# One core, five engine queues in another order: a gated recurrence with a gated convolution layer

## The chip, the cores and the metric

The kernel runs on one core of a Trainium2 chip. Its engines each work through a queue of their own in order: TensorE (PE; its weight loads are listed apart as PEld), VectorE (DVE), ScalarE (ACT), GpSimd (POOL) and SyncE (SP), which here only issues DMAs. An instruction waits at the head of its queue until the instructions that it depends on, on other engines, have signalled. The metric is the device time in microseconds (us) of one launch, as the median of several runs.

## The reference

The inputs are `x`, `r_gate` and `i_gate`, each 4 x 6336 x 256 in float32, and small weights. For every channel, with `k = 8 log(clip(sigmoid(a_param)))`:

```python
a_t = exp(k * sigmoid(r_gate))
u_t = sqrt(max(1 - a_t * a_t, 1e-6)) * sigmoid(i_gate) * x
h_t = a_t * h_(t-1) + u_t                 # along the 6336 steps of each batch
gate = sigmoid(sum_k conv_w[k] * h_(t-4+k))   # 5 taps, causal, per channel
out = (gate * (h @ w_val)) @ w_out        # both weights 256 x 256
```

The output is again 4 x 6336 x 256 in float32.

## The kernel before

The four batches are one row of 25344 steps. It is cut into 51 windows (`w`, 256 or 512 steps) and 28 chunks (`c`): chunks 0, 1, 2, 26 and 27 are one window each (0, 1, 2, 49 and 50), and every other chunk is two windows of 512 (chunk 3 is windows 3 and 4, chunk 25 is windows 47 and 48). Loads bring steps to partitions; PE transposes bring channels to partitions, in two halves (`h` 0 and 1), for the recurrence. All sigmoids are made from Tanh, so that Tanh and Exp use one activation table; Sqrt needs another, and each change between them is a table load (L501).

No scheduler decides the order. One long string, `ORDER`, names every piece of work as a word, and the loop at L496 emits the words in turn (`@` gives the PSUM banks). An engine's queue is therefore the words of that engine in the order of the string. The words, by engine:

- SP: `lr.w`, `li.w`, `lx.w` load a window of `r_gate`, `i_gate` and `x` (0.5 MB each for 512 steps); `st.w` stores a window of the output; `s_wl` loads weights.
- ACT: `th.w` Tanh of both gates of a window (L290); `ex.c.h` Exp that gives `a` for a group of one or two chunks (L342); `rt.b` Sqrt for a batch of one to three chunks (L369; batch 3 is chunks 3 and 4, batch 4 is chunks 5 to 7, batch 11 the last two); `tg.w` Tanh of the convolution (L441); `sa.c.h` a square of `a` (L358); `ca.w.0` copy of a result from PSUM (L474).
- POOL: `pp.w` adds 1 to the Tanh of the input gate, in place (L298); `up.w` multiplies that by `x` (L310); `sq.c.h` a square of `a` (L350).
- DVE: `uv.w` does both steps of `pp` and `up` at once, as two instructions of half a window each (one for 256 steps; L315); `sv.c.h` a square of `a` (L354); `xg.w` multiplies by the root (L389); `sc.c.h` the recurrence as a scan, one per half (L422); `gv.w` gate times value (L454); `cd.w.0` copy of a result from PSUM (L472).
- PE: `tr`, `nt`, `xt` transposes (L326, L382, L400); `cv.w` convolution by diagonal matrices (L434); `vl.w` and `ou.w` the two products (L449, L464).

So the gated input of a window comes from `pp` and `up` on POOL or from `uv` on DVE, and a square from `sq` on POOL, `sv` on DVE or `sa` on ACT, as `ORDER` has it.

What one window needs, in turn: `lr`, `li` -> `th` -> `tr` -> `ex` -> `sq`/`sv`/`sa` -> `rt` -> `nt`; `th` and `lx` -> `pp`, `up` or `uv`; both -> `xg` -> `xt` -> `sc` -> `cv` -> `tg` and `vl` -> `gv` -> `ou` -> `cd`/`ca` -> `st`. Buffers are rings, and a word also waits until its slot is free. The rings that matter here: `riring`, four windows (`lr.w` and `li.w` wait for `th.(w-4)`); `xring`, four windows (`lx.w` waits for the `up` or `uv` of w-4); `tring`, three windows, whose part for the input gate is single (`th.w` waits for the `up` or `uv` of w-3); `tgring`, three windows; `oring`, four windows.

The two ways to the gated input:

```python
def op_up(w):                                   # POOL, after op_pp(w)
    u, t1, xt = u_args(w)
    nc.gpsimd.tensor_tensor(out=u, in0=t1, in1=xt, op=ALU.mult)

def op_uv(w):                                   # DVE
    u, t, xt = u_args(w)
    for q in range(wins[w] // (2 * P)):
        nc.vector.scalar_tensor_tensor(out=u[:, q], in0=t[:, q], scalar=1.0, in1=xt[:, q],
                                       op0=ALU.add, op1=ALU.mult)
```

Of the kernel before, what the change touches and what calls it, by code (L numbers as in the profile page):

```python
# [532 lines left out]
```

## Time and profile before

| what | value |
|---|---|
| median of 3 runs | 303.58 us (302.06, 303.58, 303.75) |
| the profiled execution's own time | 301.82 us |
| its span (first to last instruction) | 300.0 us |
| busy: ACT, DVE, PE, POOL | 281.7, 260.6, 238.4, 209.6 us |
| moved by DMA | 104.75 MB, 349 GB/s over the span |
| ACT words: th, ex, rt, tg, sa, ca | 51, 38, 12, 51, 6, 18 |

The difference between the profiled execution's time and its span lies outside the traced instructions. "Busy" is the time in which an engine had an instruction of its own in work; starts of neighbours on one engine lie a little closer than the durations, so sums of durations come out slightly above the time that they take. A group's mean duration, the idle time before it, and what ended that idle time are what the rows of the profile give.

### The profile page before, as it was taken

To read this page: it belongs to the slowest core of one execution; us is meant where nothing else is said; L and a number is where in the kernel's file an instruction comes from. 1 tells how busy PE (TensorE), PEld (TensorE's weight loads), DVE (VectorE), ACT (ScalarE), POOL (GpSimd) and SP (SyncE) were. 2 spreads that over 40 slices of the span, in tenths; PEclk is the share of its full clock that TensorE was granted. 3 is DMA by queue.
4 is the path that set the end of the run, shared out by engine and by line. 5 is a ranking of instruction groups with operands and counts; after the bars stand their busy time and mean duration, and the time that the engine had idled before them with its cause. 6 is when DMAs were issued, how large, how long until landed. Compare 5 with 4: busy or idle time off the path is not lost.

```text
span 300.0 us, 6281 instructions
## 1 busy us (share of the span) xinstructions
PE 238.4 (79%) x2487; PEld 165.2 (55%) x2487; DVE 260.6 (87%) x241; ACT 281.7 (94%) x203; POOL 209.6 (70%) x137
## 2 busy tenths in 40 slices
...
GB/s 258 408 410 398 397 390 409 386 378 375 392 391 381 385 378 415 415 376 374 410 416 409 415 416 413 305 357 405 303 418 407 318 315 316 263 42 137 214 125 246
DMA packets 29996, 104.75 MB, mean 349 GB/s; under 512 B 3335, under 2 KB 3854, under 8 KB 29966
## 3 DMA queue, kind: packets, MB, share of 16 engines
...
q14 instruction: 11, 0.09, 0.1%
...
## 4 chain that ended last, share of the span: by engine, by line
ACT 29%; PE 24%; DVE 20%; DMA 16%; issue 9%; SPq 1%; ACTq 0%; DVEq 0%
DMA riring<-in_i_gate_dram 14%; ACT tring L290 9%; DVE yring L422 9%; PE banks L464 7%; ACT ering L369 6%; PE banks L434 6%; ACT tgring L441 6%; PE banks L449 5%; ACT aring L342 5%; DVE tgring L454 4%; PE banks L382 3%; DVE uring L389 3%; DVE oring L472 3%; PE banks L400 2%; ACT L501 2%
## 5 line engine op out<-in xcount | busy, mean ns | idle before, releaser
L350 POOL TENSOR_TENSOR ering<-aring 128x1024 f32<-128x1024 f32 (+2 forms) x48 | 85.7, 1803 | 38.9 <-ACT aring L342 38.6
L422 DVE TENSOR_TENSOR_SCAN yring<-aring,yring,banks 128x1024 bf16<-128x1024 f32 (+5 forms) x54 | 106.4, 1990 | 1.0 <-ACT aring L342 0.5
L290 ACT ACTIVATE tring<-riring 128x2048 bf16<-128x2048 f32 (+1 forms) x51 | 93.5, 1865 | 3.5 <-DMA riring<-in_i_gate_dram 2.6
L310 POOL TENSOR_TENSOR uring<-tring,xring 128x1024 bf16<-128x1024 bf16 (+1 forms) x39 | 81.7, 2110 | 3.9 <-PE banks L434 1.7
L434 PE MATMUL banks<-yring,diag 64*64 64x512 bf16 (+7 forms) x1080 | 65.5, 371 | 5.1 <-DVE oring L472 3.5
L454 DVE SCALAR_TENSOR_TENSOR tgring<-tgring,banks 128x1024 bf16<-128x1024 bf16 (+1 forms) x51 | 59.7, 1181 | 4.3 <-ACT tgring L441 2.1
L464 PE MATMUL banks<-wo,tgring 128*128 128x256 bf16 x396 | 52.1, 277 | 8.1 <-DVE tgring L454 6.2
L342 ACT ACTIVATE aring<-banks,khf 128x2048 f32<-128x2048 bf16 (+3 forms) x38 | 54.4, 1473 | 0.7 <-PE banks L326 0.6
L441 ACT ACTIVATE tgring<-banks 128x1024 bf16<-128x1024 f32 (+1 forms) x51 | 49.6, 1005 | 4.6 <-PE banks L434 3.4
L449 PE MATMUL banks<-yring,wv 128*128 128x512 bf16 (+4 forms) x216 | 51.6, 367 | 2.7 <-ACT tgring L441 0.9
L464 PEld LDWEIGHTS <-tgring 128*128 128x128 bf16 x396 | 42.0, 115 | 18.5 <-DVE tgring L454 11.1
L382 PE MATMUL banks<-ident,ering 128*128 128x128 f32 x198 | 31.7, 306 | 23.0 <-ACT ering L369 22.3
L298 POOL TENSOR_SCALAR tring<-tring 128x1024 bf16<-128x1024 bf16 (+1 forms) x39 | 39.6, 1028 | 14.2 <-ACT tring L290 14.0
L434 PEld LDWEIGHTS <-diag 64*64 64x64 bf16 x1080 | 30.0, 108 | 32.2 <-issue 17.5
L369 ACT ACTIVATE ering<-ering 128x4096 bf16<-128x4096 f32 (+5 forms) x15 | 45.0, 3019 | 0.1
L382 PEld LDWEIGHTS banks<-ident,ering 128*128 128x128 f32 x198 | 28.0, 209 | 27.5 <-ACT ering L369 23.0
L389 DVE TENSOR_TENSOR uring<-banks,uring 128x1024 bf16<-128x1024 bf16 (+1 forms) x51 | 31.8, 666 | 10.0 <-PE banks L382 9.4
L472 DVE COPY oring<-banks 128x1024 f32<-128x1024 f32 (+1 forms) x33 | 38.6, 1178 | 2.0 <-PE banks L464 1.9
L326 PE MATMUL banks<-ident_b,tring 128*128 128x128 bf16 x396 | 29.2, 229 | 13.0 <-ACT tgring L441 6.0
L326 PEld LDWEIGHTS <-tring 128*128 128x128 bf16 x396 | 25.3, 103 | 19.1 <-issue 11.8
L449 PEld LDWEIGHTS <-wv 128*128 128x128 bf16 x216 | 19.8, 99 | 23.0 <-issue 10.3
L315 DVE SCALAR_TENSOR_TENSOR uring<-tring,xring 128x512 bf16<-128x512 bf16 x23 | 17.4, 823 | 13.1 <-DMA xring<-in_x_dram 10.7
...
## 6 DMA issues: line engine op xcount, KB each, us to landing
...
```

The costliest lines, as they stand in the source:

```text
L290: nc.scalar.activation(out=tring[:, w % NTRI, a:a + 2, 0:J, :], in_=riring[:, w % NRI, :, 0:J, :], func=ACT.Tanh, scale=0.5)
L310: nc.gpsimd.tensor_tensor(out=u, in0=t1, in1=xt, op=ALU.mult)
L342: nc.scalar.activation(out=dst, in_=src, func=ACT.Exp, scale=khf[:, h:h + 1], bias=khf[:, h:h + 1])
L350: nc.gpsimd.tensor_tensor(out=e, in0=a, in1=a, op=ALU.mult)
L369: nc.scalar.activation(out=ering[:].bitcast(BF16)[:, 4 * o:4 * o + 2 * n], in_=ering[:, 2 * o:2 * o + 2 * n], func=ACT.Sqrt, scale=-0.25, ...
L382: nc.tensor.transpose(out=bank[:, (q * H + h) * P:(q * H + h + 1) * P], in_=ering[:, o + h * clen[c] // 2 + q:o + h * clen[c] // 2 + wins[ ...
L422: nc.vector.tensor_tensor_scan(out=yring[:, h, col:col + o1 - o0], data0=aring[:, h, a_at[c] + o0:a_at[c] + o1], data1=xT[:, o0:o1], initi ...
L434: nc.tensor.matmul(out=gp[oh * 64:oh * 64 + 64, h, a:b], lhsT=diag[half * 64:half * 64 + 64, h, k, :], rhs=yring[half * 64:half * 64 + 64, ...
L441: nc.scalar.activation(out=tgring[:, w % NTG, :, 0:wins[w]], in_=live.pop(("gp", w))[:, :, 0:wins[w]], func=ACT.Tanh, scale=0.5)
L449: nc.tensor.matmul(out=val[:, m, a:b], lhsT=wv[:, hk, m * P:(m + 1) * P], rhs=yring[:, hk, col:col + b - a], start=(hk == 0), stop=(hk == ...
L454: nc.vector.scalar_tensor_tensor(out=tgring[:, w % NTG, :, 0:wins[w]], in0=tgring[:, w % NTG, :, 0:wins[w]], scalar=1.0, in1=live.pop(("va ...
L464: nc.tensor.matmul(out=ops[:, j * D:(j + 1) * D], lhsT=gv[:, hk, j:wins[w]:J], rhs=wo[:, hk, :], start=(hk == 0), stop=(hk == H - 1))
```

## The change

Only the string `ORDER` changes; all functions stay as they are, `uv` and its two instructions included. The new string is a new search's result, in which the two halves of `uv` are counted as separate steps between which POOL may take its turn. It has 993 words instead of 990:

- `pp` and `up` on POOL now make the gated input of windows 3, 5, 6, 8 and 11, which `uv` on DVE made before; `uv` makes that of windows 14 and 36, which were POOL's. DVE has 9 `uv` instead of 12, POOL 42 `pp` and 42 `up` instead of 39.
- Squares: `sa.1.0`, `sa.1.1`, `sa.3.0` (ACT) and `sq.2.1`, `sq.3.1` (POOL) become `sv` (DVE); `sa.26.0` and `sa.27.0` become `sq` (POOL). ACT keeps one, `sa.27.1`.
- Copies: `ca.18`, `ca.29`, `ca.34` become `cd`; `cd.23`, `cd.31`, `cd.49` become `ca`. ACT keeps 18.
- Nearly all other words keep their engine and stand at other places, and many use other PSUM banks.

The beginning of both strings up to `rt.4` and their end, with three places between of the new one:

```diff
 ORDER = """
-s_ident s_small s_kt s_diag lr.2 li.2 th.2 tr.2.1@0 tr.2.0@1 li.0 lr.0 th.0 lr.1 li.1 th.1 tr.1.1@2 tr.0.1@3 tr.1.0@4
-ex.2.0 pp.1 ex.2.1 ex.1.0 li.3 sq.2.1 lx.0 ex.0.1 tr.0.0@1 ex.0.0 uv.0 ex.1.1 sq.2.0 sq.0.1 rt.2 sa.1.1 lx.3 lr.3
-sq.0.0 rt.0 nt.0@2 nt.2@3 xg.0 xt.0@0,1 pp.2 lx.2 sa.1.0 lx.1 lr.5 li.4 li.5 lx.4 lr.4 sc.0.0 sc.0.1 rt.1 nt.1@2 up.1
-xg.1 xt.1@0,1 th.3 up.2 xg.2 th.5 uv.3 th.4 li.6 lr.6 cv.0@2,3 tg.0 uv.4 sc.1.1 li.7 sc.1.0 th.6 tr.3.1@2,3 lr.7 lx.5
-uv.5 s_wl.3 lx.6 th.7 li.8 uv.6 ex.3.1 sv.4.1 sq.3.1 tr.3.0@0,1 ex.3.0 lr.8 th.8 lx.8 lx.7 s_wl.0 li.10 xt.2@5,4
-sc.2.0 s_wl.1 li.9 s_wl.2 lx.10 lr.10 sa.3.0 sv.4.0 rt.3 uv.8 uv.7 sc.2.1 lr.9 th.10 lr.11 nt.4@5 nt.5@0 xg.5 li.11
-th.9 lx.9 xg.4 nt.3@4 xg.3 s_wcast th.11 lr.12 uv.10 lx.11 uv.9 li.14 li.12 lr.14 lr.13 li.13 cv.1@0,1 tg.1 li.15
-lx.12 uv.11 vl.1@4,5 vl.0@2,3 gv.1 lx.13 tr.5.1@6,7 tr.5.0@0,1 ex.5.1 ex.5.0 sq.6.1 gv.0 xt.3@6,7 sc.3.0 sq.6.0 th.12
-th.14 ou.0.0@2 ou.1.0@3 cd.1.0 st.1 lr.15 nt.6@0 xg.6 sq.5.0 cd.0.0 sc.3.1 th.13 vl.2@4,5 cv.2@0,1 sq.5.1 tg.2 gv.2
-tr.7.0@2,3 st.0 pp.14 tr.7.1@0,1 cv.4@6,7 uv.12 ex.7.0 uv.13 ex.7.1 sq.7.1 th.15 ou.2.0@2,3 tg.4 xt.4@4,5 cd.2.0
-cv.3@0,1 sq.7.0 tg.3 li.16 lr.16 lx.14 lr.17 sc.4.0 rt.4 sq.8.1 pp.15 st.2 up.14 sq.8.0 li.17 lx.15 up.15 li.18 lx.16
...
-sc.23.0 sc.23.1 ou.39.0@0,1 st.37 ca.38.0 pp.47 cv.40@4,5 th.49 li.50 ca.39.0 up.47 th.50 cv.41@2,3 tg.40 cv.42@0,1
-vl.40@4,5 gv.40 lx.50 tg.41 tr.26.1@2 tg.42 nt.47@3 xg.47 vl.41@0,1 st.38 gv.41 ex.26.1 st.39 tr.27.0@2 ex.27.0
-sa.27.0 tr.27.1@7 tr.26.0@6 ex.26.0 ex.27.1 xt.24@4,5 ou.40.0@2,3 ca.40.0 ou.41.0@0,1 sc.24.1 sc.24.0 sa.26.0 ca.41.0
-sq.26.1 pp.50 pp.49 cv.44@6,7 tg.44 cv.43@2,3 vl.42@0,1 gv.42 vl.43@6,7 tg.43 gv.43 st.40 vl.44@2,3 gv.44 sa.27.1
-rt.11 xt.25@5,4 sc.25.1 sc.25.0 st.41 ou.42.0@0,1 ca.42.0 ou.43.0@6,7 ca.43.0 cv.46@2,3 tg.46 cv.45@0,1 tg.45
-vl.46@6,7 nt.49@4 ou.44.0@2,3 ca.44.0 gv.46 up.49 xg.49 nt.50@5 vl.45@0,1 ou.46.0@6,7 up.50 xt.26@2,3 xg.50 gv.45
-vl.47@4,5 sc.26.0 sc.26.1 st.42 cv.47@0,1 ca.46.0 cv.48@6,7 st.43 tg.47 gv.47 ou.45.0@0,1 st.44 vl.48@2,3 tg.48 gv.48
-cv.49@4,5 st.46 ca.45.0 st.45 tg.49 vl.49@6,7 xt.27@2,3 gv.49 ou.47.0@0,1 ca.47.0 st.47 sc.27.0 ou.48.0@4,5 sc.27.1
-ou.49.0@6,7 ca.48.0 st.48 cd.49.0 st.49 cv.50@2,3 vl.50@4,5 tg.50 gv.50 ou.50.0@4 ca.50.0 st.50
+s_ident s_small s_kt s_diag li.2 li.0 lr.0 th.0 lr.2 th.2 tr.2.1@0 lx.0 li.1 lr.1 tr.2.0@1 th.1 tr.0.1@2 ex.0.1 ex.2.1
+uv.0 pp.1 lx.1 up.1 tr.1.0@3 tr.0.0@4 tr.1.1@5 ex.0.0 lr.3 ex.2.0 sq.2.0 sq.0.1 li.3 ex.1.0 th.3 lr.4 sq.0.0 li.4 th.4
+rt.0 sv.2.1 rt.2 ex.1.1 lx.2 lx.3 li.6 nt.2@3 lr.5 li.5 pp.2 pp.3 sv.1.0 lx.4 lr.6 up.3 up.2 xg.2 th.5 nt.0@1 uv.4
+th.6 tr.3.1@2,3 li.7 lr.7 th.7 pp.5 sv.1.1 lx.5 up.5 pp.6 xg.0 ex.3.1 sv.4.1 tr.3.0@0,1 ex.3.0 li.8 lr.8 th.8 sv.4.0
+sv.3.0 lr.10 lx.7 lx.6 xt.0@4,5 sv.3.1 s_wl.0 up.6 s_wl.3 li.10 pp.8 s_wl.1 lr.9 sc.0.1 rt.1 nt.1@0 xg.1 rt.3 sc.0.0
+s_wl.2 xt.1@1,0 li.9 li.11 uv.7 lx.8 sc.1.0 lr.11 th.10 cv.0@4,5 tg.0 lx.10 lr.12 li.12 lx.9 lx.11 th.9 lr.13 li.13
+up.8 nt.3@2 xg.3 sc.1.1 th.11 nt.4@3 xg.4 lr.14 li.14 lx.12 xt.2@6,7 sc.2.0 xt.3@2,3 cv.1@4,5 tg.1 tr.5.1@0,1 ex.5.1
+nt.6@6 s_wcast sc.2.1 sc.3.1 sc.3.0 tr.5.0@4,5 ex.5.0 uv.9 lr.15 th.12 vl.0@0,1 li.15 uv.10 gv.0 th.13 nt.5@7 cv.4@2,3
+vl.1@4,5 gv.1 xg.5 pp.11 up.11 ou.0.0@0 vl.4@4,5 cd.0.0 ou.1.0@7 st.0 cd.1.0 lx.14 xg.6 th.14 tg.4 cv.2@0,1 tg.2
+tr.7.0@6,7 sq.6.0 ex.7.0 uv.12 th.15 xt.4@2,3 gv.4 sc.4.1 sc.4.0 tr.7.1@0,1 ex.7.1 vl.2@4,5 cv.3@6,7 tg.3 vl.3@2,3
+gv.2 ou.2.0@4,5 cd.2.0 sq.5.0 sq.6.1 gv.3 sq.7.0 sq.5.1 ou.4.0@6,7 ou.3.0@2,3 st.1 li.17 li.18 lx.13 uv.13 cd.4.0
+cd.3.0 uv.14 sq.7.1 rt.4 cv.5@4,5 li.16 lr.16 th.16 lr.18 sq.8.1 sq.8.0 pp.15 lx.15 up.15 nt.8@2 xg.8 st.2 lr.17 pp.16
...
+st.23 cv.26@4,5 tr.19.0@0,1 sq.18.0 sq.18.1 vl.24@2,3 tg.26 nt.29@4 sc.15.0 ex.19.0 sc.15.1 tr.19.1@5,6 ex.19.1 gv.24
+uv.36 pp.37 pp.38 xg.29 up.37 vl.25@0,1 gv.25 th.40 li.42 lx.39 cv.27@2,3 ou.24.0@6,7 cd.24.0 st.24 xt.16@5,4 sc.16.1
...
+nt.42@3 th.48 tr.25.0@2 xg.42 xt.21@4,5 tg.37 gv.37 ex.25.0 tr.25.1@3 ex.25.1 sc.21.0 sc.21.1 ou.35.0@6,7 ca.35.0
...
+xg.45 ca.38.0 nt.46@6 xg.46 nt.43@7 xg.43 up.47 vl.39@2,3 nt.44@6 tg.39 gv.39 xg.44 nt.47@7 vl.40@4,5 tg.40 gv.40
+lx.50 xg.47 ou.39.0@2,3 st.36 lr.50 xt.23@0,1 st.38 th.49 tr.26.1@6 ca.39.0 lx.48 ex.26.1 sq.26.1 st.39 th.50
+cv.41@4,5 tg.41 cv.42@6,7 tg.42 ou.40.0@2,3 ca.40.0 st.40 vl.42@4,5 vl.41@6,7 tr.27.1@2 sc.23.0 sc.23.1 xt.24@0,3
+ex.27.1 tr.27.0@1 tr.26.0@2 gv.42 ex.27.0 sa.27.1 pp.48 ou.42.0@4,5 nt.48@1 ca.42.0 up.48 st.42 sq.27.0 gv.41 sc.24.1
+ou.41.0@6,7 ca.41.0 st.41 ex.26.0 cv.44@4,5 sq.26.0 pp.49 up.49 xg.48 tg.44 sc.24.0 cv.43@6,7 tg.43 rt.11 vl.43@2,3
+gv.43 vl.44@4,5 gv.44 xt.25@6,7 sc.25.1 sc.25.0 cv.46@0,1 cv.45@2,3 tg.45 ou.43.0@4,5 ca.43.0 nt.49@7 xg.49 st.43
+tg.46 ou.44.0@2,3 ca.44.0 vl.45@4,5 st.44 cv.47@0,1 tg.47 pp.50 gv.45 vl.46@2,3 gv.46 up.50 ou.45.0@4,5 ca.45.0 st.45
+xt.26@0,1 sc.26.1 vl.47@6,7 gv.47 cv.48@2,3 tg.48 ou.46.0@4,5 nt.50@1 vl.48@6,7 ou.47.0@2,3 sc.26.0 ca.46.0 st.46
+ca.47.0 st.47 xg.50 xt.27@4,5 cv.49@0,1 tg.49 vl.49@2,3 gv.48 ou.48.0@6,7 ca.48.0 sc.27.1 st.48 sc.27.0 cv.50@0,1
+tg.50 gv.49 ou.49.0@2,3 ca.49.0 st.49 vl.50@6,7 gv.50 ou.50.0@6 ca.50.0 st.50
 """
```

More of the change, by code (lines that the diff above doesn't have):

```diff
@@ new lines @@
+uv.36 pp.37 pp.38 xg.29 up.37 vl.25@0,1 gv.25 th.40 li.42 lx.39 cv.27@2,3 ou.24.0@6,7 cd.24.0 st.24 xt.16@5,4 sc.16.1
+ou.25.0@0,1 tg.27 cd.25.0 st.25 lx.38 lr.42 lr.41 li.41 cv.28@2,3 vl.26@6,7 gv.26 lx.40 sq.19.0 lx.41 th.39 li.43
+lr.43 sc.16.0 vl.27@0,1 gv.27 sq.19.1 sq.17.1 sq.17.0 tg.28 vl.28@2,3 ou.26.0@6,7 gv.28 rt.8 lr.44 li.44 cd.26.0
+cv.30@4,5 ou.27.0@0,1 cd.27.0 tg.30 nt.31@2 xg.31 tr.21.1@3 ex.21.1 tr.21.0@6 ex.21.0 st.26 st.27 nt.33@7 xg.33
+nt.32@0 xg.32 nt.34@4 xg.34 vl.30@1,2 gv.30 xt.17@7,0 sc.17.1 cv.29@4,5 ou.28.0@2,3 pp.40 sq.20.1 sc.17.0 sq.20.0
```

77 lines of the change are left out of this document (34 added, 43 removed).

## The prediction

> **What bounds the kernel now.** I read the page's busy times first, then busy times by stretches of 30 us, then ACT, DVE and POOL in order of time in three places: the start, the words that collide, and the end.
>
> The page, busy time by engine:
>
> ```profile
> span 300.0 us, 6281 instructions
> ...
> PE 238.4 (79%) x2487; PEld 165.2 (55%) x2487; DVE 260.6 (87%) x241; ACT 281.7 (94%) x203; POOL 209.6 (70%) x137
> ```
>
> ACT has 18.3 us of idle time in all, DVE 39.4, POOL 90.4. The stretches say where (columns: stretch, length, busy us of PE, PEld, DVE, ACT, POOL, then granted clock, DMA share, GB/s):
>
> ```profile
> 0.00:30.00 30.00, 10.80 (x87) 8.32 (x87) 10.48 (x23) 26.15 (x27) 9.09 (x15) 1.00 0.95 368
> 30.00:60.00 30.00, 13.49 (x117) 9.61 (x118) 24.44 (x26) 27.31 (x16) 14.79 (x10) 0.72 1.03 396
> ...
> 120.00:150.00 30.00, 27.29 (x281) 19.38 (x279) 29.38 (x26) 29.94 (x20) 29.66 (x20) 1.00 1.01 393
> ...
> 240.00:270.00 30.00, 28.22 (x310) 19.83 (x304) 29.02 (x23) 29.30 (x27) 21.27 (x14) 1.00 0.67 234
> 270.00:300.00 30.00, 25.16 (x264) 16.22 (x256) 22.11 (x20) 19.48 (x21) 1.23 (x2) 0.96 0.45 181
> ```
>
> From 60 to 270 us ACT is idle for 1.3 us in all: its queue sets the time there, with DVE close behind. ACT's idle time lies in the first 60 us (6.5 us) and the last 30 (10.5). A new order of the same work can win only there, or lose anywhere.
>
> The start, by order of time (start, length, engine, line, operation, count):
>
> ```profile
> 30.87 2.14 POOL L350 TENSOR_TENSOR ering<-aring 128x1024 f32<-128x1024 f32 x1 [11.98 <-ACT aring L342]
> 31.19 2.91 DVE L354 TENSOR_TENSOR ering<-aring 128x1024 f32<-128x1024 f32 x1
> ...
> 35.21 1.19 DVE L354 TENSOR_TENSOR ering<-aring 128x1024 f32<-128x1024 f32 x1
> ...
> 51.09 7.91 POOL L350 TENSOR_TENSOR ering<-aring 128x1024 f32<-128x1024 f32 x4 [10.25 <-ACT aring L342]
> ...
> 70.01 5.42 ACT L369 ACTIVATE ering<-ering 128x4096 bf16<-128x4096 f32 x2
> ```
>
> The same square on DVE (L354) takes 1.19 us alone and 2.91 beside a POOL square: it begins 0.32 us after POOL's, and ends about one own length after POOL's end. The instructions of the gated input on DVE (L315; shortest, median, longest ns) tell the same:
>
> ```profile
> L315 DVE SCALAR_TENSOR_TENSOR uring<-tring,xring x23: 720/736/2435, 10.9 to 64.1; 128x512 bf16<-128x512 bf16 x23
> ```
>
> The one of 2.435 us is the second half of uv.11, beside the POOL squares that begin at 51.09: blocked for 1.7 us. The Trainium skill has this as a rule ("SBUF — State Buffer", section "Who interferes with whom"): a DVE instruction with two SBUF inputs contends with a GpSimd instruction that reads SBUF, and the one that starts second waits for all of the other. Both rows agree, and the rule speaks against this change, which puts more such squares on DVE. By the rule taken everywhere, all six halves of uv.9, uv.10 and uv.12 would be blocked, 10 us on DVE; by the rows, where 2 of 25 such instructions were blocked, it is one or none, and I go by the rows.
>
> The end (DVE, and ACT's last):
>
> ```profile
> 275.44 4.58 DVE L422 TENSOR_TENSOR_SCAN yring<-aring,yring,banks 128x1024 bf16<-128x1024 f32 x2
> ...
> 286.45 1.22 DVE L454 SCALAR_TENSOR_TENSOR tgring<-tgring,banks 128x1024 bf16<-128x1024 bf16 x1 [0.73 <-ACT tgring L441]
> 288.60 1.22 DVE L454 SCALAR_TENSOR_TENSOR tgring<-tgring,banks 128x1024 bf16<-128x1024 bf16 x1 [0.93 <-ACT tgring L441]
> 290.68 1.22 DVE L454 SCALAR_TENSOR_TENSOR tgring<-tgring,banks 128x1024 bf16<-128x1024 bf16 x1 [0.86 <-PE banks L400]
> ...
> 293.42 1.23 DVE L472 COPY oring<-banks 128x1024 f32<-128x1024 f32 x1 [0.22 <-PE banks L464]
> 294.73 0.69 DVE L454 SCALAR_TENSOR_TENSOR tgring<-tgring,banks 128x512 bf16<-128x512 bf16 x1
> 296.13 0.59 ACT L474 COPY oring<-banks 128x512 f32<-128x512 f32 x1 [1.43 <-PE banks L464]
> ```
>
> sc.25.0, the second scan of the first row, ends at 280.0. From there to gv.50's end at 295.4 stand 13.0 us of DVE rows and about 3 us of waits; then ca.50 ends at 296.7 and the store takes until 300.0.
>
> **The parts, by queue.** ACT loses five squares: sa.1.0 and sa.1.1 (0.42 us each), sa.3.0 (1.05), sa.26.0 (0.63), sa.27.0 (0.42): -2.9 us. Both orders have 20 table loads (1.28 each) in the loop over words and 18 copies. DVE loses uv.3, 5, 6, 8, 11 (1.46 us each) and gains uv.14 and uv.36, and the squares sv.2.1, 1.0, 1.1, 3.0, 3.1: about 3.8 us alone, from the 1.19 us row by size, and up to 1.7 more for each that meets a POOL instruction. POOL gains three net of pp with up (1.05 + 2.16 each) and loses and gains some squares: +8.3 us. These lie before 55 us, where POOL's waits of 11.98 and 10.25 us (first and fourth row above) cover them. Without that cover they would delay rt.4, at 1 us for 1 us.
>
> The rest only changes places. So I lay each queue of the new order end to end with the mean durations of the rows, less the overlap of neighbours (0.085 us per ACT row, 0.09 per DVE row: starts in the profile are that much closer than the durations). The same done on the order before, from rt.4's start at 70.0, puts rt.11 at 274.1 (the profile: 273.7) and, with DVE's waits for ACT added, sc.25.0 within 0.2 us. That is the accuracy I claim for it.
>
> *Start to rt.4.* Loads land at 0.5 MB per 1.26 us. ACT runs as before up to th.8 (end 34.5; before 34.5), since th.7 waits for the same 9 MB. Then rt.3 waits for four DVE squares in a row: sv.4.1 from 31.4, sv.4.0 from 32.7, and then up.6 (2.16 us, its x lands near 34) comes between. Unblocked, rt.3 starts at 36.4, with one POOL instruction between at 38.2, with two at 39.5; before it was 36.8. I take 38.2: up.6 is due just then. After it th.10, tg.0, th.9, th.11, tg.1, both ex.5, th.12 to th.14, tg.4, tg.2, ex.7.0, th.15, ex.7.1, tg.3 follow without a wait if uv.9, uv.10 and uv.12, which free their tring slots for th.12, th.13 and th.15, aren't blocked: rt.4 at 69.5, against 70.0. The order before had ACT waits of 1.2 us (before th.11) and 1.3 us (before tg.2) in this stretch; that they go pays for the later rt.3. Bounds: 68.0 (no block at all) to 75 (four blocked halves of uv, 1.7 each, less what ACT's waits absorb).
>
> *rt.4 to tg.37.* 95 ACT words, 181.5 us by rows, 173.2 with the overlaps: tg.37 ends at 242.7. Nothing in it comes due before its inputs: the nearest are up.32 for th.35 and up.27 for th.30, 0.4 and 0.5 us early, as near as before (up.35 for th.38: 0.0). Loads land 3 us or more ahead of their th, laid at 0.5 MB per 1.27 us behind the word that frees their slot. The last load on SP's queue is now lx.48, which waits for up.44: it lands near 260, up.48 ends by 263, and xg.48 stands at 270. uv.14 and uv.36, each blocked twice, would hold DVE 3.4 us near 74 and 185 us; but DVE's waits for ACT add up to 7.7 us by tg.37 and only to 5 near 185, which absorbs most of it.
>
> *tg.37 to the end.* gv.37 follows tg.37 and DVE then sets the pace: 26 DVE words to sc.25.0, 39.8 us by rows, 37.4 with overlaps: sc.25.0 ends at 280.2, against 280.0. From there DVE has 11.8 us of rows instead of 13.0, because cd.49 (1.23) goes to ACT, and waits near 2.6 us, chiefly for cv.47, cv.49 and vl.50. gv.50 ends at 293.6, ca.50 at 295.0 instead of 296.7.
>
> Sum: -0.5 at rt.4, given back by the denser DVE stretch (+0.2 at sc.25.0), -1.9 after it and +0.2 for ACT's ending: **-1.7 us**. ACT's queue alone gives nearly the same: -0.5 and 1.0 us less work from rt.4 on. The profiled execution took 301.82 us with a span of 300.0; 1.7 less is 300.1. The median of the runs before is 1.76 above it, so as a median I forecast **301.9**.
>
> **Rivals.**
>
> *Slower: DVE's two-input words meet POOL.* In the new order POOL runs sq.6.0, sq.5.0, sq.6.1 back to back from about 53 us, and uv.9, uv.10, uv.12 stand on DVE right there, each in two halves. Every half that comes second waits up to 1.7 us (uv.11's row), behind it DVE's sc, gv and xg, and ACT's th.12, th.13 and th.15. One such half cancels the forecast's gain; three make 3 × 1.7 - 1.7 = +3.4 us: 307.0. For it: the two rows of 2.91 and 2.435. Against it: before, uv.12 and uv.13 met none, and POOL's squares wait for ex.5 and ex.7, with gaps between.
>
> *Faster by over 1%: the start is freed.* If no square is blocked, rt.3 comes at 36.4 and rt.4 near 68.0, 1.5 earlier than I take, and ACT carries it through to the end; a tail with 2 us of waits instead of 2.6 adds 0.6: 299.8. For it: DVE squares of 1.19. Against it: up.6 due at 34.
>
> *The change moves nothing:* PE, whose queue I did not lay end to end, holds the same places as before; the last 20 us are PE's by the chain (a run of 0.9 us pieces of PE from 255 to 293), and cd.49's move is hidden under its waits: 303.5.
>
> **Chances.** Forecast 0.42, moves nothing 0.14, faster rival 0.18, slower rival 0.26. One per cent is 3 us, about what a measurement of this kernel can tell (its three runs spread over 1.7). Hence faster by over 1% 0.18, within 0.56, slower 0.26. The range goes from 299.0, just under the faster rival, to 308.5, about four blocked halves (+5.1); outside are some 0.08 below and 0.1 above. The forecast's own range is 300.6 to 303.2.
>
> **What would show it.** Right: ACT's first 4096-wide Sqrt (rt.3) near 38.2 and the second start of that form (rt.4) near 69.5; no ACT wait over 1 us from 75 to 245; L354 rows on DVE between 1.2 and 2.9; the last ACT copy ends near 295. Wrong: L315 rows of over 2 us between 50 and 62, ACT waiting there for DVE (the slower rival); or rt.4 as said and ACT waits for PE banks later, which would mean that PE's order, not laid here, decides.

## The result, and the profile after

| | before | after |
|---|---|---|
| median of 4 runs each, same chip | 302.82 us (300.99 to 303.75) | 313.51 us (311.7 to 314.28) |
| ratio | 1 | 1.035, 95% interval 1.030 to 1.041 |
| span of the profiled execution | 300.0 us | 312.5 us |

The changed order is 3.5% slower; the forecast was 301.9. Medians in this document are of all runs, and ratios leave out runs that lie over 1.5% above the fastest of the same kernel, which are three of a7_free's ten and two of h4_loads' twelve, further down. The page after (busy time by engine):

```profile
span 312.5 us, 6233 instructions
...
PE 238.6 (76%) x2460; PEld 166.2 (53%) x2487; DVE 272.2 (87%) x240; ACT 280.8 (90%) x198; POOL 220.5 (71%) x143
```

ACT has one microsecond less work and 31.7 us of idle time instead of 18.3. DVE shows 11.6 us more busy time with one instruction less: the instructions are longer, not more. The stretches (columns as before):

```profile
0.00:30.00 30.00, 8.43 (x59) 6.76 (x59) 7.97 (x15) 24.88 (x23) 14.02 (x18) 1.00 0.96 371
30.00:60.00 30.00, 13.35 (x132) 9.78 (x132) 27.13 (x22) 23.80 (x15) 19.63 (x14) 0.72 0.99 382
120.00:150.00 30.00, 26.52 (x303) 18.52 (x308) 29.70 (x26) 29.94 (x20) 29.73 (x18) 1.00 1.01 392
240.00:270.00 30.00, 27.64 (x310) 19.33 (x315) 28.93 (x28) 29.78 (x21) 22.96 (x14) 1.00 0.87 316
```

The middle is as full as before; between 30 and 60 us ACT is busy for 23.8 us instead of 27.3. There the timeline shows (DVE, POOL, ACT):

```profile
52.12 9.34 DVE L315 SCALAR_TENSOR_TENSOR uring<-tring,xring 128x512 bf16<-128x512 bf16 x4
...
51.80 2.15 POOL L310 TENSOR_TENSOR uring<-tring,xring 128x1024 bf16<-128x1024 bf16 x1 [1.35 <-DMA xring<-in_x_dram]
53.90 6.97 POOL L350 TENSOR_TENSOR ering<-aring 128x1024 f32<-128x1024 f32 x3
...
56.92 1.91 ACT L290 ACTIVATE tring<-riring 128x2048 bf16<-128x2048 f32 x1 [3.22 <-issue]
61.49 3.71 ACT L290 ACTIVATE tring<-riring 128x2048 bf16<-128x2048 f32 x2 [2.66 <-DVE uring L315]
...
76.66 3.62 ACT L369 ACTIVATE ering<-ering 128x4096 bf16<-128x4096 f32 x1
```

The four halves of uv.9 and uv.10 take 9.34 us instead of 4 × 0.74 = 2.9: they begin 0.3 us after up.11 and then lie beside the squares sq.6.0, sq.5.0 and sq.6.1. th.12 and th.13 wait for them, and rt.4 starts at 76.7 instead of 70.0. (The profile names no releaser for th.12's 3.22 us, but th.12 starts 0.1 us after the second half of uv.9 ends, at 56.84.) The same line over the whole run:

```profile
L315 DVE SCALAR_TENSOR_TENSOR uring<-tring,xring x17: 710/739/2416, 8.4 to 197.0; 128x512 bf16<-128x512 bf16 x17
```

Its median and longest are as before (736 and 2435); what changed is how many are long: eight of 17 take over 1.5 us, where before it was one of 23. The two other long places, uv.13 and uv.36, with the ACT words that waited behind them, tg.6 and tg.28:

```profile
70.76 9.35 POOL L350 TENSOR_TENSOR ering<-aring 128x1024 f32<-128x1024 f32 x5 [9.89 <-ACT aring L342]
78.63 3.52 DVE L315 SCALAR_TENSOR_TENSOR uring<-tring,xring 128x512 bf16<-128x512 bf16 x2
91.04 1.02 ACT L441 ACTIVATE tgring<-banks 128x1024 bf16<-128x1024 f32 x1 [1.23 <-PE banks L434]
...
194.65 8.38 POOL L350 TENSOR_TENSOR ering<-aring 128x1024 f32<-128x1024 f32 x4 [0.92 <-ACT aring L342]
195.01 4.45 DVE L315 SCALAR_TENSOR_TENSOR uring<-tring,xring 128x512 bf16<-128x512 bf16 x2
204.93 1.02 ACT L441 ACTIVATE tgring<-banks 128x1024 bf16<-128x1024 f32 x1 [3.52 <-PE banks L434]
```

The profile puts both waits of ACT down to PE (L434, the convolution). PE itself had waited for DVE words that stood behind uv: 3.49 us until 84.5 for the copies cd.4 and cd.3 (L472), and 2.22 us until 200.1 for xg.29 (L389). The words of PE between that second wait and cv.28 are xt.16 and ou.25:

```profile
200.08 1.88 PE L400 MATMUL banks<-ident,uring 128*128 128x128 f32 x8 [2.22 <-DVE uring L389]
201.75 1.91 PE L464 MATMUL banks<-wo,tgring 128*128 128x256 bf16 x8
```

From 200.2 to 203.6 us the granted clock, the share of its full speed that the profile shows for PE, was 0.50. In h3_uv36_early and a7_free below, where uv.36 isn't blocked, the same two words take 1.04 us each at a clock of 1.00. So about 1.7 us of tg.28's 3.52 are PE's slower pace right behind its wait.

### The profile page after: what moved, and what is told of

Read it like the earlier page. It is cut to its first block, busy times and chain, and to the rows that moved or that the text cites. A ratio compares the mean times of both kernels' runs of the same rounds, so it can differ in the third digit from the quotient of the medians.

```text
span 312.5 us, 6233 instructions
## 1 busy us (share of the span) xinstructions
PE 238.6 (76%) x2460; PEld 166.2 (53%) x2487; DVE 272.2 (87%) x240; ACT 280.8 (90%) x198; POOL 220.5 (71%) x143
## 4 chain that ended last, share of the span: by engine, by line
PE 24%; DVE 19%; DMA 8%; POOL 8%; ACT 7%; issue 6%; SPq 1%; DVEq 0%; ACTq 0%
DVE yring L422 9%; PE banks L434 6%; PE banks L449 6%; PE banks L464 5%; DVE oring L472 4%; PE banks L382 4%; DMA riring<-in_r_gate_dram 3%; DVE tgring L454 3%; ACT tring L290 3%; POOL uring L310 3%; DMA xring<-in_x_dram 3%; POOL ering L350 2%; DMA riring<-in_i_gate_dram 2%; POOL tring L298 2%; PE banks L326 2%
## 5 line engine op out<-in xcount | busy, mean ns | idle before, releaser
L310 POOL TENSOR_TENSOR uring<-tring,xring 128x1024 bf16<-128x1024 bf16 (+1 forms) x42 | 88.9, 2122 | 24.4 <-DMA xring<-in_x_dram 22.9
L434 PE MATMUL banks<-yring,diag 64*64 64x512 bf16 (+7 forms) x1080 | 63.8, 368 | 3.5 <-DVE oring L472 2.1
L464 PE MATMUL banks<-wo,tgring 128*128 128x256 bf16 x396 | 53.4, 280 | 15.1 <-DVE tgring L454 14.2
L298 POOL TENSOR_SCALAR tring<-tring 128x1024 bf16<-128x1024 bf16 (+1 forms) x42 | 44.3, 1063 | 18.4 <-ACT tring L290 17.4
L449 PE MATMUL banks<-yring,wv 128*128 128x512 bf16 (+7 forms) x189 | 48.8, 362 | 7.7 <-DVE yring L422 2.9
L382 PE MATMUL banks<-ident,ering 128*128 128x128 f32 x198 | 33.2, 310 | 24.7 <-ACT ering L369 18.1
L382 PEld LDWEIGHTS banks<-ident,ering 128*128 128x128 f32 x198 | 28.7, 208 | 30.6 <-ACT ering L369 10.8
L434 PEld LDWEIGHTS <-diag 64*64 64x64 bf16 x1080 | 28.7, 108 | 28.6 <-issue 13.3
L389 DVE TENSOR_TENSOR uring<-banks,uring 128x1024 bf16<-128x1024 bf16 (+1 forms) x51 | 32.5, 664 | 10.8 <-POOL uring L310 7.7
L472 DVE COPY oring<-banks 128x1024 f32<-128x1024 f32 (+1 forms) x33 | 38.4, 1179 | 4.1 <-PE banks L464 3.3
L326 PE MATMUL banks<-ident_b,tring 128*128 128x128 bf16 x396 | 30.2, 230 | 10.4 <-ACT tring L290 8.1
L400 PE MATMUL banks<-ident,uring 128*128 128x128 f32 x198 | 29.4, 293 | 4.9 <-DVE uring L389 4.4
```

The source lines that it names most:

```text
L326: nc.tensor.transpose(out=bank[:, o:o + P], in_=tring[:, w % NTRI, 2 * swapped(w), j, h * P:(h + 1) * P], identity=ident_b[:])
L382: nc.tensor.transpose(out=bank[:, (q * H + h) * P:(q * H + h + 1) * P], in_=ering[:, o + h * clen[c] // 2 + q:o + h * clen[c] // 2 + wins[ ...
L434: nc.tensor.matmul(out=gp[oh * 64:oh * 64 + 64, h, a:b], lhsT=diag[half * 64:half * 64 + 64, h, k, :], rhs=yring[half * 64:half * 64 + 64, ...
L449: nc.tensor.matmul(out=val[:, m, a:b], lhsT=wv[:, hk, m * P:(m + 1) * P], rhs=yring[:, hk, col:col + b - a], start=(hk == 0), stop=(hk == ...
L464: nc.tensor.matmul(out=ops[:, j * D:(j + 1) * D], lhsT=gv[:, hk, j:wins[w]:J], rhs=wo[:, hk, :], start=(hk == 0), stop=(hk == H - 1))
L472: nc.vector.tensor_copy(out=dst, in_=src)
```

## The experiments

All runs in one table. "Ratio" is to the kernel before on the same chip (its medians there: 301.85 to 303.13 us). The starts of rt.4 and tg.7 and the span are those of the profiled execution, which is a single run: that of after took 314.28 us, 0.8 above the median, that of a5 310.05, 1.5 above, that of h2 305.07, 1.7 below. Kernels run on different chips are compared by their ratios, since the medians of before differ by up to 1.3 us.

| kernel | median us | ratio, 95% interval | rt.4 | tg.7 | span |
|---|---|---|---|---|---|
| before | see ratio | 1 | 70.0 | 88.0 | 300.0 |
| after | 313.51 | 1.035 (1.030 to 1.041) | 76.7 | 96.6 | 312.5 |
| a1_uv_early | 312.43 | 1.035 (1.030 to 1.040) | 72.6 | 92.4 | 309.8 |
| a2_uv36_pool | 313.30 | 1.038 (1.032 to 1.044) | 75.5 | 95.4 | 310.4 |
| a3_both | 311.02 | 1.030 (1.025 to 1.035) | 72.5 | 92.5 | 308.5 |
| h1_start_after | 311.88 | 1.028 (1.023 to 1.033) | 76.6 | 98.6 | 310.8 |
| h2_start_before | 306.72 | 1.011 (1.005 to 1.018) | 69.5 | 87.4 | 303.3 |
| b1_uv_late | 309.38 | 1.020 (1.015 to 1.025) | 78.0 | 95.9 | 307.7 |
| b2_uv_late | 307.00 | 1.013 (1.008 to 1.018) | 75.7 | 93.6 | 305.3 |
| t1_tail | 302.49 | 0.999 (0.995 to 1.002) | 70.1 | 88.1 | 300.9 |
| a4_uv13 | 319.84 | 1.053 (1.044 to 1.061) | 84.0 | 101.9 | 317.7 |
| a5_x9 | 308.54 | 1.015 (1.008 to 1.022) | 69.0 | 93.5 | 308.2 |
| a6_all | 315.79 | 1.041 (1.034 to 1.048) | 79.4 | 97.3 | 312.8 |
| h3_uv36_early | 306.20 | 1.011 (1.007 to 1.016) | 69.6 | 88.7 | 304.7 |
| a7_free | 305.28 | 1.007 (1.003 to 1.011) | 69.3 | 87.2 | 303.3 |
| h4_loads | 304.30 | 1.004 (1.000 to 1.008) | 69.3 | 87.8 | 301.9 |
| a8_loads | 306.33 | 1.013 (1.008 to 1.017) | 69.9 | 88.2 | 304.6 |

### The disputed cost by itself

p1_port runs eight instructions of one kind on DVE and eight on POOL, alone and side by side.

> The meeting alone, without the rest: bursts of 8 equal instructions on DVE and on POOL. In this order: uv halves alone; POOL squares alone; uv halves beside squares; DVE squares beside POOL squares; gv-like DVE instructions (one input in PSUM) beside squares; uv halves beside pp; uv halves beside up. Theory A: uv halves 0.73 us alone; beside squares each ends one own length after a POOL square, so that a pair takes about 0.73 + 1.9 = 2.6 us and both engines take turns; gv beside squares is unchanged at 1.2. Rival: the two share the port by halves, and both slow by a part with no steps. It computes nothing of the reference.

Timeline, DVE and POOL. L56 is a half of uv, L66 POOL's square, L60 DVE's square and L63 the form of gv, with one input in PSUM; the first two rows are alone, the last two stand beside pp and beside up, the others beside POOL's squares:

```profile
9.15 5.76 DVE L56 SCALAR_TENSOR_TENSOR ut<-gt,xt 128x512 bf16<-128x512 bf16 x8
15.53 15.68 POOL L66 TENSOR_TENSOR et<-at 128x1024 f32<-128x1024 f32 x8
31.88 17.98 POOL L66 TENSOR_TENSOR et<-at 128x1024 f32<-128x1024 f32 x8
32.10 18.32 DVE L56 SCALAR_TENSOR_TENSOR ut<-gt,xt 128x512 bf16<-128x512 bf16 x8
51.35 22.46 DVE L60 TENSOR_TENSOR ot<-at 128x1024 f32<-128x1024 f32 x8
74.61 15.68 POOL L66 TENSOR_TENSOR et<-at 128x1024 f32<-128x1024 f32 x8
74.82 9.99 DVE L63 SCALAR_TENSOR_TENSOR ut<-gt,ps 128x1024 bf16<-128x1024 bf16 x8
91.17 11.34 DVE L56 SCALAR_TENSOR_TENSOR ut<-gt,xt 128x512 bf16<-128x512 bf16 x8
103.34 20.10 DVE L56 SCALAR_TENSOR_TENSOR ut<-gt,xt 128x512 bf16<-128x512 bf16 x8
```

A half of uv takes 0.72 us alone and 2.29 beside squares (18.32 / 8), and POOL's square 2.25 instead of 1.96: the two take turns, one of each per 2.3 us. Theory A of the expectation holds, with 2.3 us a pair instead of 2.6. Beside pp a half takes 1.4 us, beside up 2.5. Each pair costs about 0.35 to 0.4 us less than both lengths added. gv's form takes 1.25 us each (1.2 in the kernel) and leaves POOL untouched, 15.68 us in all. So a blocked half of uv costs DVE about 1.6 us more beside a square, and POOL 0.3.

### One collision taken away, then the other

```diff
 # a1_uv_early (DVE order): both uv ahead of the scans of chunk 3
-sc.2.1 sc.3.1 sc.3.0 uv.9 uv.10
+sc.2.1 uv.10 uv.9 sc.3.1 sc.3.0
 # a2_uv36_pool
-uv.36
+pp.36 up.36
 # a3_both: both edits
```

> The changed kernel with uv.10 and uv.9 moved on DVE's queue ahead of sc.3.1, where POOL has no squares to run; nothing else. Theory A (a two-input DVE instruction that meets a POOL instruction waits for all of it, and the wait passes to ACT through th.12 and th.13): the four halves take about 3 us instead of 9.3, th.12 starts near 54 instead of 56.9, rt.4 near 70.5 instead of 76.7, and the span falls from 312.5 by about 6 to 306.5. Theory B (the blocked halves only fill time in which DVE would have waited anyway, and the loss comes from the order of PE's words and its banks): rt.4 comes earlier, but the span stays above 311.

> The changed kernel with uv.36 undone: pp.36 and up.36 on POOL stand in its place. Theory A: uv.36's 4.45 us on DVE go, ACT's wait of 3.5 us before tg.28 goes with them, and the span falls by about 3 to 309.5, less what POOL's 3.2 us more cost. Theory B: POOL is as full as DVE there, and the span stays within 1 us of 312.5.

> Both of the last two edits. Theory A: the two prices add, about 9 us, span near 303.5 and a ratio to the kernel before near 1.01. Theory B: above 310.

In a1 the two uv ran unblocked, with other waits in their place (DVE):

```profile
47.88 1.36 DVE L315 SCALAR_TENSOR_TENSOR uring<-tring,xring 128x512 bf16<-128x512 bf16 x2
50.96 1.35 DVE L315 SCALAR_TENSOR_TENSOR uring<-tring,xring 128x512 bf16<-128x512 bf16 x2 [1.73 <-DMA xring<-in_x_dram]
...
59.71 0.69 DVE L454 SCALAR_TENSOR_TENSOR tgring<-tgring,banks 128x512 bf16<-128x512 bf16 x1 [2.36 <-PE banks L449]
```

9.34 us became 2.7, and rt.4 came 4.1 us earlier, not 6.4: uv.9 now waits for its x, and gv.1 for vl.1, which stands behind cv.4 on PE. In after itself vl.1 was done by 54.6 us and x had landed, so these two waits come from the new place of uv. By the ratios nothing was won, 1.035 both, which is nearer to theory B's time than to theory A's. In the trace a1 is ahead of after by 3.9 us until ex.17.1 and by 2.7 from ex.17.0 on, which waits 1.09 us for PE in a1 and not at all in after. In a2, whose ratio of 1.038 isn't below after's, tg.28's wait goes, but th.40 waits for POOL instead, and rt.8 for another 0.57 us:

```profile
197.72 1.91 ACT L290 ACTIVATE tring<-riring 128x2048 bf16<-128x2048 f32 x1 [2.36 <-POOL uring L310]
```

POOL is as full as DVE there, so the work can't simply go back to it. a3's ratio is 1.030 against 1.035, with overlapping intervals, and its span of 308.5 lies between what the two theories said. The collision of uv.9 and uv.10 is not the whole loss.

### Which part of the order carries the loss

h1 has the changed order up to rt.4 and the words of the order before behind it; h2 the other way round.

```diff
 # h1_start_after: the words of after up to rt.4, then those of before not yet emitted
 # h2_start_before: the words of before up to rt.4, then sc.4.1 and those of after not yet emitted
```

> The changed order up to rt.4, then the words of the order before for all the rest (uv.14 already done, li.16, lr.16 and lr.17 first). Theory S (the loss lies in the start alone: rt.4 comes 6.7 us later than before, and every later stage hands that on, because DVE and ACT have no slack to win it back): rt.4 near 76.7, the rest as before behind it, median near 302.8 + 6.7 = 309.5, so 1.5 to 2.5% over the kernel before. Theory R (the rest of the new order loses as much by itself, and before's rest has slack that absorbs the late start): median under 306.

> The order before up to rt.4, then the words of the changed order for all the rest (pp.14 with up.14 instead of uv.14; sc.4.1 stands first, so that its bank is free). Theory S: rt.4 near 70, and the rest costs what the start left over: median near 303 to 304. Theory R: the rest of the new order loses 3 to 5 us by itself (uv.36 beside POOL, the end): median 306 to 308.

The start alone costs 8.9 us (h1), the rest alone 3.7 (h2); together they would make 12.6 against 10.7 measured. From tg.7 on, every ACT word of after stands 8.9 to 9.2 us behind the same word of h2 in the two profiled executions, to the end: nothing is won back. And h2's own loss is one place (DVE, ACT):

```profile
185.83 4.45 DVE L315 SCALAR_TENSOR_TENSOR uring<-tring,xring 128x512 bf16<-128x512 bf16 x2
...
195.70 1.02 ACT L441 ACTIVATE tgring<-banks 128x1024 bf16<-128x1024 f32 x1 [3.48 <-PE banks L434]
```

It is uv.36 again, with rt.4 at 69.5, where the prediction had it; no other wait of ACT between 75 and 265 us is over 0.45 us. The spans differ by 3.3 us from before.

### One part alone in the order before

```diff
 # b1_uv_late (order before): uv.10 and uv.9 moved behind sc.3.0
-uv.10 lx.11 uv.9 ... sc.3.0 sq.6.0 th.12
+lx.11 ... sc.3.0 uv.9 uv.10 sq.6.0 th.12
 # b2_uv_late: and lx.13 moved from ahead of tr.5.1 to behind uv.10
 # t1_tail (order before)
-sa.27.0 ... sa.26.0 ... sq.26.1 ... cd.49.0 st.49 cv.50 vl.50 tg.50
+sq.26.1 sq.27.0 sq.26.0 ... cv.50 vl.50 tg.50 ca.49.0 st.49
```

> The order before with one thing altered: uv.9 and uv.10 stand on DVE behind sc.3.0, beside POOL's squares from 51 us on, instead of before gv.1 (44 to 50 us), where POOL is idle. Theory of the collision (the four halves take turns with POOL's squares, 2.3 us a pair instead of 0.72, and nothing absorbs it): the two uv take 6 to 9 us instead of 2.9, th.12 and th.13 wait for them, rt.4 4 to 6 us later, median near 307. Rival (the slack in the start absorbs it, or the halves fall into gaps between the squares): rt.4 within 1.5 us of 70.0, median under 304.5.

> As b1_uv_late, with lx.13 also moved behind uv.10 on SP, so that uv.9 reads its own x and waits for no later load. Theory of the collision: uv.9 and uv.10 stand beside POOL's squares from 57 us on, or meet their tail; they take 4 to 9 us instead of 2.9, th.12 and th.13 wait for them, rt.4 comes 3 to 6 us later than 70.0, median 305 to 308. Rival: the halves fall behind the squares, which end near 59.5, and the slack of the start absorbs the move: rt.4 within 1.5 us, median under 304.5.

> The order before with only the new order's changes of engine at the end: sq.26.0 and sq.27.0 on POOL instead of sa on ACT, and ca.49 on ACT behind tg.50 instead of cd.49 on DVE. By the prediction's last step: ACT has 1.05 us less before rt.11 and DVE 1.2 less before gv.50, so the end comes 1 to 1.9 us earlier, median near 301.3. Rival (PE sets the last 20 us, and tg.50 waits for its banks either way): within 0.5 us of the kernel before.

b1 measured something else: lx.13 came to stand ahead of uv.9, so that window 9 was made with the x of window 13, and uv.9 waited 3.63 us for that load. b2 mends this:

```profile
57.03 4.36 DVE L315 SCALAR_TENSOR_TENSOR uring<-tring,xring 128x512 bf16<-128x512 bf16 x4
...
60.24 5.51 ACT L290 ACTIVATE tring<-riring 128x2048 bf16<-128x2048 f32 x3 [7.16 <-DVE uring L315]
```

The four halves take 4.36 us instead of 2.6 (they meet only the end of the squares), and rt.4 comes 5.7 us later, the end of the span 5.3, the median 3.9. Less than 2 us of it is blocking; the rest is that uv stands later, and th.12 waits for that. Both runs show what the hybrids show: a delay of rt.4 (8.0 and 5.7 us) reaches the end of the profiled span nearly in full (7.7 and 5.3).

t1 moves nothing that can be told from zero (the interval leaves room for a gain of 1.4 us): the last gv (gv.50) now waits 1.53 us for tg.50 in place of cd.49, and tg.50 still waits for PE. The rival of its expectation fits better than a gain of 1 to 1.9 us.

### The other collisions of the start

```diff
 # all on a3_both
 # a4_uv13: lx.13 behind cd.1.0; uv.13 and uv.14 behind uv.12
-uv.12 th.15 ... st.1 li.17 li.18 lx.13 uv.13 cd.4.0 cd.3.0 uv.14
+lx.13 lx.14 ... uv.12 uv.13 uv.14 th.15 ... st.1 li.17 li.18 cd.4.0 cd.3.0
 # a5_x9: lx.9 behind lx.10; cv.4 behind gv.1
-lx.10 lr.12 li.12 lx.9 ... cv.4@2,3 vl.1@4,5 gv.1
+lx.10 lx.9 lr.12 li.12 ... vl.1@4,5 gv.1 cv.4@2,3
 # a6_all: both
```

> a3_both with uv.13 and uv.14 right behind uv.12 on DVE (near 64.6 us, where POOL is idle, instead of 75.8 beside its squares), and lx.13 ahead of lx.14 on SP. Theory of the collision: both uv take 1.4 us, xg.10 and xg.11 come 1.5 to 2 us earlier, tg.6's wait of 1.46 us goes, and the end comes 2 us earlier than a3_both (311.0): near 309. Rival (DVE's total of work from 60 us on decides, and only the 0.9 us of blocking is won): at most 1 us.

> a3_both with lx.9 right behind lx.10 on SP, ahead of lr.12 and li.12, and cv.4 behind vl.1 and gv.1 on PE's queue instead of ahead of vl.1. Theory (what is left of the late start is DVE waiting for x of window 9, 2.1 us, and for PE's vl.1 behind cv.4, 2.6 us): both waits go, rt.4 comes 2 to 4 us earlier than a3_both's 72.5, and the end as much: 307 to 309. Rival (tg.4 and the loads of r and i take over the wait): rt.4 within 1 us of 72.5, median above 310.

> a4_uv13 and a5_x9 together. If the start's loss consists of these waits, the gains add: 305.5 to 307, near h2_start_before (306.7), and what stays is what the rest of the new order costs (3.3 us by the spans). Rival (the new start puts too much of DVE's work behind 38 us, whatever the waits): 308.5 or more.

a4 went the wrong way by 8.8 us in the medians, 7 by the ratios. x of window 13 landed late, so uv.13 waited, and then all four halves met POOL's squares of chunks 5, 7 and 8 (DVE, POOL):

```profile
67.83 9.06 DVE L315 SCALAR_TENSOR_TENSOR uring<-tring,xring 128x512 bf16<-128x512 bf16 x4 [2.35 <-DMA xring<-in_x_dram]
...
67.49 11.12 POOL L350 TENSOR_TENSOR ering<-aring 128x1024 f32<-128x1024 f32 x5 [7.06 <-ACT aring L342]
```

The expectation had POOL idle there, and it was, until 0.3 us before. rt.4 came 11.5 us later: 6.4 for the four blocked halves, 2.4 for the load, and 2.7 for the unblocked length of two uv. They now stand ahead of gv.4, for which PE waits 10.95 us before vl.2, and behind vl.2 come cv.3 and tg.3, ahead of rt.4 on ACT. a6, which has this too, shows the same loss less a5's gain; neither came near its expectation.

a5 takes away the waits that a1's new place of uv had brought, and did what it was to do: rt.4 at 69.0, and a median of 308.54, within the 307 to 309 expected (ratio 1.015 after a3's 1.030). Yet in its profiled execution tg.7 comes 1.1 us later than in a3, and the span is only 0.3 us shorter. The reason is in the next 20 us (DVE, then ACT):

```profile
72.57 4.06 DVE L315 SCALAR_TENSOR_TENSOR uring<-tring,xring 128x512 bf16<-128x512 bf16 x2
...
78.78 4.14 DVE L315 SCALAR_TENSOR_TENSOR uring<-tring,xring 128x512 bf16<-128x512 bf16 x2
...
82.95 1.91 ACT L290 ACTIVATE tring<-riring 128x2048 bf16<-128x2048 f32 x1 [2.54 <-DVE uring L315]
...
88.66 1.02 ACT L441 ACTIVATE tgring<-banks 128x1024 bf16<-128x1024 f32 x1 [2.88 <-PE banks L434]
```

uv.13 and uv.14, now earlier, both lie beside POOL's pp, up and squares: 8.2 us instead of 2.7, and ACT waits for them twice.

### The costly collisions taken away

```diff
 # h3_uv36_early (on h2): uv.36 ahead of gv.24, into 0.9 us of POOL's idle time
-sc.15.1 ... gv.24 uv.36
+sc.15.1 uv.36 ... gv.24
 # a7_free (on after): uv.10, uv.9, lx.9, cv.4 as in a5; uv.36 as in h3; and
-sq.6.1 ... uv.13 ... uv.14 sq.7.1 rt.4 ... sq.8.1 sq.8.0 pp.15 ... up.16
+sq.6.1 pp.13 pp.14 ... sq.7.1 up.13 up.14 rt.4 ... pp.15 ... up.16 sq.8.1 sq.8.0
```

> h2_start_before with one word moved: uv.36 ahead of gv.24 on DVE instead of behind it, 1.1 us earlier, into the 0.9 us in which POOL waits for sq.18.0's input. In h2 it took 4.45 us beside POOL's squares, tg.28 waited 3.48 us, and that is ACT's only long wait between 75 and 265 us. Theory of the collision: uv.36 takes 1.4 to 2.2 us, tg.28's wait falls under 1 us, the span goes from 303.3 to about 300.5, and the median is within 0.4% of the kernel before. Rival (the rest of the new order loses by something else, and a wait of like size comes up behind): span above 302.

> The changed order with every collision of uv taken away: uv.10, uv.9, lx.9 and cv.4 as in a5_x9, the input of windows 13 and 14 made on POOL (pp.13, pp.14 ahead of sq.7.0, up.13, up.14 behind sq.7.1, sq.8.1 and sq.8.0 behind up.16), and uv.36 ahead of gv.24 as in h3. Theory of the collision (a5's rt.4 came at 69.0, and what it lost again before tg.7 was uv.13 and uv.14, 8.2 us instead of 2.7): tg.6 near 83.5 without a wait over 1 us, rt.5 near 98 to 99, the span 300 to 303, median 302 to 305. Rival (the new start leaves DVE more work whatever collides): tg.7 above 91, median above 307.

In a7 one uv is still long, uv.12 with 2.58 us beside pp.13 and pp.14, but th.15 behind it starts 1.3 us after its end, so that nothing waits for it. ACT doesn't wait for tg.6: tg.7 comes at 87.2, 9.4 us earlier than in after, and by the ratios the kernel is about 2.7% faster than after and 0.7% slower than before. In h3 one word moved 1.1 us on its queue (DVE, ACT):

```profile
189.35 1.33 DVE L315 SCALAR_TENSOR_TENSOR uring<-tring,xring 128x512 bf16<-128x512 bf16 x2
...
197.11 1.02 ACT L441 ACTIVATE tgring<-banks 128x1024 bf16<-128x1024 f32 x1
```

uv.36 takes 1.33 us instead of 4.45, and tg.28 (second row) waits for nothing. Against h2's words, h3 stands 4.5 us behind just before this place and 1.4 behind after it: 3.1 us won. But its ratio is h2's, 1.011, and the expectation (within 0.4% of before) failed: the profiled execution had waited 1.8 us for loads at th.21 and th.20, and 1.1 for PE at an Exp near 176 us. a7 shows such a wait for a load too (th.21):

```profile
93.24 3.71 ACT L290 ACTIVATE tring<-riring 128x2048 bf16<-128x2048 f32 x2 [2.18 <-DMA riring<-in_r_gate_dram]
```

### What is left: loads behind waiting stores

In the new order's rest st.2, st.3 and st.4 stand on SP's queue ahead of loads of windows 17 to 21, and wait for DVE's copies.

```diff
 # h4_loads (on h3), a8_loads (on a7): SP's queue only
-st.2 ... lx.16 ... st.3 st.4 lx.18 lr.19 lr.20 li.19 lx.17
+lx.16 lr.19 li.19 st.2 ... lx.17 lx.18 st.3 st.4 lr.20
```

> h3_uv36_early with only SP's queue altered: lr.19, li.19 ahead of st.2, and lx.17, lx.18 ahead of st.3 and st.4 (stores that wait for DVE's copies near 75 us and hold the loads behind them). In h3's profiled run th.19 to th.21 waited 1.8 us for these loads and the run stood 3.1 us later than h2's profiled run by th.20. Theory L (in the new order the loads behind waiting stores land just in time or late, and that is what stays when the collisions are gone): no wait of ACT for a DMA from 75 to 100 us, median 302 to 304, within 0.5% of the kernel before. Rival (the late loads are an effect of a single execution): median as h3, 306.2.

> a7_free with the same alteration of SP's queue. Theory L: ACT's 2.18 us wait for lr.21 at 93 us goes, the span falls from 303.3 to 300.5 to 301.5, the median from 305.3 to 302.5 to 303.5, so that the new order, mended, comes within 0.5% of the kernel before. Rival: median above 304.5.

In h4 the waits for loads between 75 and 100 us are gone, and it is 0.4% above before (interval 0.0 to 0.8%), where h3 was 1.1% (0.7 to 1.6): for theory L, though the intervals overlap and the median of 304.3 is just above the 302 to 304 expected. In a8 the wait at 93 us is gone as well, but its ratio is 1.013 against a7's 1.007, and theory L's median (302.5 to 303.5) is missed. The gain was turned into a wait for POOL's squares, which pp and up of windows 13 and 14 have made late (rt.5):

```profile
99.51 5.33 ACT L369 ACTIVATE ering<-ering 128x6144 bf16<-128x6144 f32 x1 [1.42 <-POOL ering L350]
```

Between rt.6 and rt.7 a8 loses another 0.7 us to a7, with a wait of 0.56 us for POOL in it; no run tried that.

The Exp of h3 near 176 us is ex.17.0. The same wait for PE, 1.0 to 1.1 us, stands in eight of the twelve profiled executions with the new order's rest (a1, a3, a4, a6, a7, a8, h3, h4), each time 3 to 5 us after a stretch of 3.4 us with a granted clock of 0.50; in the other four (after, a2, a5, h2) both are absent, though PE waits 1.52 us for a scan there in all twelve. So this wait alone makes about 1 us between the spans of single executions.

No version was measurably faster than the kernel before.

## Why the prediction was wrong, point by point

The mechanism was in the text as the slower rival, with its words (uv.9, uv.10, the squares of chunks 5 and 6, th.12 and th.13). It was priced at three blocked halves (307.0) where eight were blocked, and given 0.26, and the time lies outside the range.

**Start to rt.4, up to 52 us: right, and for the reason given.** rt.3 started at 38.4 (38.2 was said): the three squares behind sv.4.1 took 5.43 us, with up.6 on POOL beside the last of them. From there to ex.5.0 at 51.6 ACT has no wait, as the lay had it.

**"By the rows ... it is one or none, and I go by the rows": the step that failed.** All four halves of uv.9 and uv.10 were blocked, for 6.4 us, and rt.4 came 7.2 us later than the 69.5 of the sum. That 2 of 25 instructions were blocked before was a property of the old order, which has these words at 44 to 50 us, where POOL has no square, pp or up (its idle time of 10.25 us ahead of 51.09); it was no rate that a new order inherits:

```profile
44.29 1.35 DVE L315 SCALAR_TENSOR_TENSOR uring<-tring,xring 128x512 bf16<-128x512 bf16 x2
47.95 1.35 DVE L315 SCALAR_TENSOR_TENSOR uring<-tring,xring 128x512 bf16<-128x512 bf16 x2 [2.31 <-DMA xring<-in_x_dram]
```

(Three more halves, of uv.8 and uv.7, stood beside POOL's weight casts at 36 us and took 0.81 to 0.93 us; the count took them as free.) The new queues were already laid end to end in the prediction; to read off which DVE words lie beside a POOL word was the missing step. The Trainium skill has the rule ("SBUF — State Buffer", section "Who interferes with whom"): two SBUF inputs on DVE contend with a GpSimd instruction that reads SBUF, and the later one waits for all of the other. The trace agrees with it for uv.9 and uv.10, 2.4 us a half. uv.12 (1.35 us for both halves) ran while POOL was idle, so that four of the six halves were blocked. The price of this step is 4.1 us at rt.4 by a1, which brings other waits in; a5, which takes those away, has rt.4 at 69.0, where the sum said 69.5.

**The bound of 75 for rt.4** took off "what ACT's waits absorb". Measured was 76.7; the new order had put th.12 and th.13 right behind these uv, so there was nothing to absorb it. Behind them ACT even waited 0.51 and 0.91 us more for PE, which had stood 7.46 us for gv.0 behind uv.10; the granted clock was 0.50 from 56.9 to 67.1 us (in before from 55.2 to 58.6).

**"DVE's waits for ACT ... absorb most of it": failed.** uv.13 was blocked for 2.2 us (2.0 later by tg.7), uv.36 for 3.1 (3.6 later at tg.28). h2 shows that this wasn't a consequence of the late start: with rt.4 at 69.5, uv.36 cost the same 3.5 us. A sum of waits up to a point says nothing of one word in it; the chain uv.36, xg.29, xt.16, ou.25, cv.28, tg.28 had less slack than the sum, and PE added about 1.7 us to it at a clock of 0.50, which the prediction did not reckon with. h3 shows it from the other side: uv.36 moved by 1.1 us, 3.1 us won.

**The end: sign right, size wrong.** From sc.25.0's end to gv.50's end 13.4 us were said, against 15.4 before; measured were 15.0 (293.2 to 308.2). t1, with these changes alone, gave nothing that its interval tells from zero. The term of the sum was the length of cd.49, and waits of 2.6 us; the waits were 3.7. What paces the end is PE, for which tg.50 waits in t1 and ca.48, right ahead of tg.50, in after, as the "moves nothing" rival had it. (The terms that the recorded sum lists make -1.5 us; its -1.7 is that of ca.50's end, 295.0 against 296.7.)

**The sum by places:** 7.2 at rt.4, 2.0 more by tg.7, 3.6 at tg.28 and a remainder of about 1.4, most of it at the end, make 14.2, the distance from the forecast span (298.3) to 312.5.

**"PE's order decides" would have been a misreading.** The prediction said that ACT waits for PE banks behind rt.4 would point to PE's order. They came, and PE, the last to signal, had itself waited for DVE (3.49 and 2.22 us). Its own part was the pace behind these waits: the granted clock was 0.50 from 84.2 to 87.6 and from 200.2 to 203.6 us.

**Left open:** of the start's loss, a7 recovers all but 2 us at rt.5 (99.2 against h2's 97.2); late loads account for that wait by the trace, but a8 could not confirm it by the time. h1 loses 4 us more between rt.4 and rt.5 than its late start; uv.13, blocked there as well, and tg.6's wait of 2 us were seen, but no run took them away. What the granted clock adds to each collision was read from the traces at tg.28 alone, and no run separates it.
